# A buffer of its own for the second half of the first block's heads, and an early exponential

## The chip, the cores and the metric

The kernel runs on one core of one Trainium2 chip. The metric is the device time of one execution in microseconds (us). The engines are TensorE (PE in the rows, its weight loads PEld), VectorE (DVE), ScalarE (ACT), GpSimd (POOL) and SyncE (SP), whose queue issues all loads and stores here.

## The reference

Three layers follow each other on 8 batches of 576 tokens, all in float32:

```python
# 1: attention in chunks of 64 tokens, 8 heads of 64
scores = scale * q_c @ k_c^T
attn = exp(scores - max(scores)); attn /= sum(attn) + 1e-9
out = attn @ v_c                        # then heads side by side: x (B, S, 512)
# 2: feed-forward with a gate
h = relu(x @ w_in)                      # 1024 features
gate = sigmoid(conv over 3 tokens of h, with conv_w)
x = (h * gate) @ w_out
# 3: Fourier mixing
u = x + real(fft2(x));  un = (u - mean) / sqrt(var + 1e-6)
y = u + relu(un @ w_ch1) @ w_ch2
```

## The kernel before, in words

The 4608 tokens are cut into ten blocks, a first one of 256 tokens, eight of 512 and a last one of 256. For each block, `attention(i, q, ...)` (line 371) is called twice, for q = 0 and q = 1: each call covers half of the heads. It loads queries and keys, lets TensorE write the scores to PSUM (line 393), takes their maxima on VectorE (line 398) and turns them into a bias (line 399). ScalarE then runs one exponential for each of the n chunks and each of two groups, with the sum accumulated beside it (line 404; n is 4 in the first block and 8 in a wide one). VectorE adds the 1e-9, inverts the sums and scales the exponentials (lines 408 to 410), TensorE transposes them (line 419), ScalarE copies the result to `at` (line 422), and TensorE multiplies with the values (line 436). ScalarE copies that to `gl` in the first block (line 443).

The feed-forward layer goes feature group by feature group (`m_step`, eight groups f to a block): the linear step into PSUM (line 460 in the first block, in float32; line 469 later, with weights and data split in a high and a low part), ReLU to `h` (line 494), the convolution (lines 499 and 489) and the gate (line 506) in a tile `cv`, and the product `gh` (line 508). `x_step` multiplies with w_out (line 532 in the first block, line 538 later).

The weights are loaded as 64-bit words of 512 KB a tile and turned into float32 by one ScalarE instruction (line 293) and three of VectorE (lines 294 to 296). The wide tiles of the first loads lie in buffers that are used for other things later, so a row may call one `dd`, `fw` or `wide`, and the float32 result `t`, `u` or `f`. Splitting into high and low parts is lines 280 and 281.

Nothing in the program is issued in the order in which the Python code stands. Each step is an `op` with an engine, an estimated cost and a due time (`prio`). `Plan.emit` (line 156) runs a clock for each engine, and each time issues, of the steps that can start first, the one that is due first. Loads are given a time of arrival by bytes at 280 per ns, one behind the other (line 194), and TensorE costs are doubled in the first 30 us of that clock (line 190). The resulting order is fixed for each engine's queue; on the chip, engines work their queues in order and wait for each other.

A buffer (`buf(pool, tag, bufs, shape)`) is one use of a ring of `bufs` tiles with the same tag. A new use of a tile must wait for the readers of the use that lies `bufs` before it in that ring. Before the change, exponentials `es`, maxima `mx` and sums `sm` have rings of one tile each; `cv` has a ring of two tiles of 128 x 512.

Of the kernel before, what the change touches and what calls it, by code (L numbers as in the profile page):

```python
# [8 lines left out]
F32 = mybir.dt.float32  # L9
# [3 lines left out]
ACT = mybir.ActivationFunctionType  # L13
# [88 lines left out]
class Plan:  # L102
# [10 lines left out]
    def buf(self, pool, tag, bufs, shape, dtype=F32):  # L113
        return Buf(self, pool, tag, bufs, shape, dtype)

    def op(self, eng, cost, fn, prio, r=(), w=(), after=(), nbytes=0, spare=0):
        o = Op()
        o.spare = spare
        o.eng, o.cost, o.fn, o.prio, o.nbytes, o.seq = eng, cost, fn, prio, nbytes, len(self.ops)
        o.slots = [b for b in w if b.tag in self.ANY_ORDER and not b.writers]  # L120
        deps = {}
        for b in r:
            assert b.writers and not b.closed, b.tag
            for d in b.writers:
                deps[d] = True
        for b in w:
            assert not b.closed, b.tag
            if not b.writers:
                if b.pool in self.opened:
                    deps[self.opened[b.pool]] = True  # L130
                if b.before is not None:
                    for d in b.before.writers + b.before.readers:
                        deps[d] = True
                if b.previous is not None and b.previous not in w:
                    deps.setdefault(b.previous.writers[0], False)
            for d in b.writers + b.readers:
                deps[d] = True
        for d in after:
            deps[d] = True
        for b in r:  # L140
            for x in (b, b.base) if b.base else (b,):
                x.readers.append(o)
        for b in w:
            for x in (b, b.base) if b.base else (b,):
                x.writers.append(o)
        o.held = [b for b in {id(b): b for b in (*r, *w)}.values() if b.tag in self.ANY_ORDER]
        for b in o.held:
            b.left += 1
        o.deps, o.users = deps, []
        for d in deps:  # L150
            d.users.append(o)
        o.left, o.ready, o.end = len(deps), 0.0, None
        self.ops.append(o)
        return o
# [73 lines left out]
def kernel(  # L228
# [15 lines left out]
    pe, dve, act, pool, sp = nc.tensor, nc.vector, nc.scalar, nc.gpsimd, nc.sync  # L244
    plan = Plan()
    buf, op = plan.buf, plan.op
# [4 lines left out]
    const = ctx.enter_context(tc.tile_pool(name="const", bufs=1))  # L251
# [4 lines left out]
    pools["s"] = tc.alloc_tile_pool(name="seq", bufs=1, side="right")  # L256

    ident = const.tile([128, 128], F32, name="ident")

    def dram_buf(name, cols=512):  # L260
        b = buf("dram", name, 1, None)
        b.tile = dram.tile([128, cols], F32, name=name, tag=name)
        return b
# [6 lines left out]
    def load(dst, src, nbytes, prio, r=(), after=()):  # L270
        return op("SP", 450, lambda: sp.dma_start(out=dst(), in_=src()), prio, r=r, w=[dst], after=after, nbytes=nbytes)

    def vop(n, fn, prio, r, w, fast=False, scalars=0):
        return op("DVE", dve_cost(n, fast, scalars), fn, prio, r=r, w=w)

    def aop(n, fn, prio, r, w, psum=False, scalars=0, after=()):
        return op("ACT", act_cost(n, psum, scalars), fn, prio, r=r, w=w, after=after)
# [93 lines left out]
    def attention(i, q, prio, last):  # L371
        nw = SIZE[i] // 256
        n = 4 * nw
        blk = AT[i] // 256
        half = (slice(0, 64), slice(64, 128))
        qks, v = [], []
        for p in range(2):
            qks.append(buf(*(("s", "xlo", 2) if i + q == 1 and not i else ("a", "qk", 2)), [128, nw, 2, 256]))
            load(qks[p], lambda p=p: qk[blk:blk + nw, 2 * q + p].rearrange("w r a t -> r w a t"), 262144 * nw, prio - 12 + p)
        for p in range(2):  # L380
            v.append(buf("a", "v", 4, [128, nw, 256]))
            load(v[p], lambda p=p: v_in[blk:blk + nw, 2 * q + p].rearrange("w r t -> r w t"), 131072 * nw, prio - 10 + p)

        s = [buf("ps", "o" if i else "x", 4, [128, n, 64]) for _ in range(2)]

        def qk_unit():
            for w in range(nw):
                for j in range(2):
                    for p in range(2):
                        for u in range(2):  # L390
                            for h in range(2):
                                t, ks = qks[p](), slice(64 * (2 * j + u), 64 * (2 * j + u) + 64)
                                pe.matmul(s[h]()[half[u], 4 * w + 2 * p + j, :], t[half[h], w, 0, ks], t[half[h], w, 1, ks], start=True, stop=True)  # L393

        op("PE", 310 + 470 * nw, qk_unit, prio, r=qks, w=s)
        es, mx, sm = buf("a", "es", 1, [128, 2 * n, 64]), buf("a", "mx", 1, [128, 2, n]), buf("a", "sm", 1, [128, 2 * n, 1])
        for h in range(2):
            vop(64 * n, lambda h=h: dve.tensor_reduce(out=mx()[:, h, :], in_=s[h](), op=ALU.max, axis=AX.X), prio, [s[h]], [mx])
        vop(2 * n, lambda: dve.tensor_scalar(mx(), mx(), -0.125, None, op0=ALU.mult), prio, [mx], [mx])  # L399

        for h in range(2):
            def exp(ks, h=h):
                for k in ks:
                    act.activation(out=es()[:, n * h + k, :], in_=s[h]()[:, k, :], func=ACT.Exp, scale=0.125, bias=mx()[:, h, k:k + 1], accum_out=sm()[:, n * h + k, :])  # L404

            for ks in (range(k, k + 4) for k in range(0, n, 4)):
                op("ACT", 291 * 4, lambda exp=exp, ks=ks: exp(ks), prio, r=[s[h], mx], w=[es, sm])
        vop(2 * n, lambda: dve.tensor_scalar(sm(), sm(), 1e-9, None, op0=ALU.add), prio, [sm], [sm])
        vop(2 * n, lambda: dve.reciprocal(out=sm(), in_=sm()), prio, [sm], [sm])
        vop(128 * n, lambda: dve.tensor_tensor(es(), es(), sm().to_broadcast([128, 2 * n, 64]), op=ALU.mult), prio, [es, sm], [es])  # L410

        at = buf("a", "at", 2, [128, n, 128])
        for c in range(nw):
            tps = buf("ps", "o", 4, [128, 4, 128])

            def tr_unit(c=c, tps=tps):
                flat = es().rearrange("p a k -> p (a k)")
                for k in range(4):
                    pe.transpose(tps()[:, k, :], flat[:, 512 * c + 128 * k:512 * c + 128 * k + 128], ident)  # L419

            op("PE", 436, tr_unit, prio + 2, r=[es], w=[tps], spare=1)
            aop(512, lambda c=c, tps=tps: act.copy(out=at()[:, 4 * c:4 * c + 4, :], in_=tps()), prio + 2, [tps], [at], True)

        return lambda: values(i, q, nw, v, at, last)
# [616 lines left out]
    for q in range(2):  # L1041
        attention(0, q, -10 + q, -6 + q)()
# [8 lines left out]
    for i in range(NBLK):  # L1051
        t, u, step = place(i, 0), place(i + 1, 0) if i + 1 < NBLK else 0, SIZE[i] / 288
        if i + 1 < NBLK:
            rest = [attention(i + 1, q, *((t + (u - t) * (0.05 + 0.4 * q), u - 1.5 + 0.3 * q) if i else (t - 3.5 + 3 * q, t + 0.5 + 3 * q))) for q in range(2)]
            if not i:
                heads(1)
                for finish in rest:
                    finish()
# [54 lines left out]
    for c in range(NCH):  # L1113
        t = start + span * c
        begun = []
        for g in range(FG):
            begun.append(group(c, g, t + 7 * g))
            if (c, g) in LATE:
                n = LATE.index((c, g))
# [8 lines left out]
            second(c, j, t + 7 * (TILE0[c] // 2 + j), c + j == 0, c == NCH - 1 and j == HT[c] - 1)  # L1128

    with tc.manual_schedule():  # L1130
        make_identity(nc, ident)
        plan.emit()
        pools["e"].tile([128, 24], F32, tag="pad", name="pad", bufs=1)
        pools["e"].release()
        pools["b"].release()
# [109 lines left out]
```

## Time and profile before

| what | value |
|---|---|
| median of 3 runs | 1303.25 us (1302.99 to 1304.23) |
| the profiled execution | 1303.06 us |
| its span | 1301.3 us |
| TensorE busy | 1274.9 us, 98% |
| VectorE busy | 1036.1 us, 80% |
| ScalarE busy | 761.4 us, 59% |
| DMA | 206.16 MB, mean 158 GB/s |

The profiled execution's time is a little longer than its span, the time from the first to the last thing that the profiler saw. The busy time of an engine counts its instructions, not its waits. The chain that ended last is followed backwards from the last instruction, at each step to what released it or to the instruction before it on its engine. In a timeline, the bracket at a row's end gives the time that the engine sat idle before it, and what ended that.

### The profile page before, as it was taken

What the parts mean: (1) busy time and instruction counts of PE and PEld (TensorE: products, weight loads), DVE (VectorE), ACT (ScalarE), POOL (GpSimd) and SP (SyncE); (2) the same over time, 40 slices, a digit from 0 to 9 for tenths busy, and PEclk for the clock granted to TensorE, in tenths of its full rate; (3) what the DMA queues carried; (4) which work ended last, traced back from release to release, by engine and by line L of the source; (5) the groups of instructions that cost most, each with busy time, mean ns of one, the idle gap of its engine ahead of it and who ended that gap; (6) DMA issues with size and microseconds to landing.
All of it is one profiled execution on the core that took longest, in us unless ns stands there. A gap on an engine that the chain in (4) does not pass through costs nothing.

```text
span 1301.3 us, 24089 instructions
## 1 busy us (share of the span) xinstructions
PE 1274.9 (98%) x8880; PEld 1106.4 (85%) x8880; DVE 1036.1 (80%) x1909; ACT 761.4 (59%) x1902; POOL 112.3 (9%) x247
## 2 busy tenths in 40 slices
PE   5899999999999999999999999999999999999998
PEld 4788888888888888999999888888888888888887
DVE  5998878888786877887977757664599998998995
ACT  6887666768676665666756556566644334334331
POOL 0131212121030312210000000000000000000000
PEclk9999999999999999999999999999999999999999
DMA  9535242534413132258674866778655554554541
GB/s 339 178 108 175 78 129 90 187 100 158 135 57 103 34 98 62 63 172 267 203 238 144 255 182 204 214 238 273 200 159 165 176 168 146 173 171 141 174 140 41
DMA packets 155319, 206.16 MB, mean 158 GB/s; under 512 B 10304, under 2 KB 103104, under 8 KB 155200
## 3 DMA queue, kind: packets, MB, share of 16 engines
q1 hardware_dynamic: 155200, 204.61, 49.7%
q8 instruction: 70, 1.15, 0.4%
q14 instruction: 49, 0.40, 0.1%
HBM read 130.51 MB, written 74.06 MB: 157 GB/s over the span
## 4 chain that ended last, share of the span: by engine, by line
PE 93%; DVE 5%; ACT 1%; issue 1%; DMA 0%; SPq 0%; DVEq 0%; ACTq 0%
PE x L946 21%; PE x L1010 15%; PE x L538 15%; PE o L469 14%; PE o L1010 12%; PE o L946 4%; PE o L672 3%; PE o L705 2%; PE o L727 1%; PE o L436 1%; PE o L393 1%; PE o L844 1%; PE o L419 1%; ACT es L404 1%; DVE cv L489 0%
## 5 line engine op out<-in xcount | busy, mean ns | idle before, releaser
L946 PE MATMUL x<-sxh,t 128*128 128x512 f32 (+1 forms) x960 | 285.2, 369 | 1.1 <-ACT sum L929 0.6
L280 ACT CAST sxh<-raw 128x1024 fp32r<-128x1024 f32 (+1 forms) x143 | 144.9, 1029 | 201.7 <-DVE raw L856 84.3
L946 PEld LDWEIGHTS x<-sxh,t 128*128 128x128 f32 x960 | 177.9, 188 | 24.9 <-ACT sum L929 1.4
L946 PE MATMUL x<-sxl,t 128*128 128x512 f32 (+1 forms) x480 | 176.3, 367 | 0.0
L281 DVE TENSOR_TENSOR sxl<-raw,sxh 128x1024 fp32r<-128x1024 f32 (+1 forms) x143 | 168.7, 1192 | 9.5 <-ACT sxh L280 9.3
L469 PE MATMUL o<-x,wih 128*128 128x512 f32 (+1 forms) x576 | 172.2, 382 | 0.0
L489 DVE SCALAR_TENSOR_TENSOR cv<-h,cw,cv 128x512 f32<-128x512 f32 (+30 forms) x272 | 129.1, 495 | 31.9 <-ACT cv L499 31.6
L1010 PE MATMUL x<-t,sxh 128*128 128x512 f32 x576 | 144.4, 392 | 0.0
L469 PEld LDWEIGHTS o<-x,wih 128*128 128x128 f32 x576 | 104.6, 188 | 19.6
L1010 PEld LDWEIGHTS x<-t,sxh 128*128 128x128 f32 x576 | 103.7, 189 | 18.5
L538 PE MATMUL x<-gh,woh 128*128 128x512 f32 (+1 forms) x288 | 112.4, 390 | 0.0
L538 PE MATMUL x<-gh,wol 128*128 128x512 f32 (+1 forms) x288 | 109.3, 379 | 0.0
L538 PE MATMUL x<-gl,woh 128*128 128x512 f32 (+1 forms) x288 | 109.2, 379 | 0.0
L469 PE MATMUL o<-x,wil 128*128 128x512 f32 (+1 forms) x288 | 108.9, 378 | 0.0
L1010 PE MATMUL o<-t,sxh 128*128 128x512 f32 x432 | 108.3, 392 | 0.0
L946 PEld LDWEIGHTS x<-sxl,t 128*128 128x128 f32 x480 | 90.2, 188 | 11.2
L1010 PEld LDWEIGHTS o<-t,sxh 128*128 128x128 f32 x432 | 77.8, 189 | 13.9
L404 ACT ACTIVATE es<-o,mx 128x64 f32<-128x64 f32 x272 | 84.0, 358 | 8.9 <-DVE mx L399 8.9
L1030 DVE TENSOR_TENSOR u<-x,u 128x256 f32<-128x256 f32 x144 | 60.4, 422 | 29.9 <-PE x L1010 28.2
L856 DVE TENSOR_TENSOR raw<-raw 128x1024 f32<-128x1024 f32 (+1 forms) x70 | 84.0, 1202 | 0.1
L1010 PEld LDWEIGHTS x<-t,sxl 128*128 128x128 f32 x576 | 78.6, 190 | 5.6
L1010 PE MATMUL x<-t,sxl 128*128 128x256 f32 x576 | 80.5, 282 | 0.0
(263 smaller groups left out, 2394.1 us busy)
## 6 DMA issues: line engine op xcount, KB each, us to landing
raw<-h_scr SPq DMA_DIRECT2D x72, 512.0 KB, 4.6
h_scr<-sum SPq DMA_DIRECT2D x72, 256.0 KB, 3.3
u<-u_scr SPq DMA_DIRECT2D x66, 256.0 KB, 3.8
qk<-in_qk SPq DMA_DIRECT2D x32, 512.0 KB, 4.9
h_scr<-sum SPq DMA_DIRECT2D x48, 192.0 KB, 2.7
out_y<-u SPq DMA_DIRECT2D x35, 256.0 KB, 2.3
v<-in_v_in SPq DMA_DIRECT2D x32, 256.0 KB, 4.4
wide<-in_w_ch SPq DMA_DIRECT2D x16, 512.0 KB, 5.1
```

The costliest lines, as they stand in the source:

```text
L280: aop(n, lambda: act.copy(out=cut(h()), in_=cut(src())), prio, [src], [h], psum, after=after)
L281: vop(n, lambda: dve.tensor_tensor(cut(l()), cut(src()), cut(h()).bitcast(F32), op=ALU.subtract), prio, [src, h], [l])
L404: act.activation(out=es()[:, n * h + k, :], in_=s[h]()[:, k, :], func=ACT.Exp, scale=0.125, bias=mx()[:, h, k:k + 1], accum_out=sm()[:, n ...
L469: pe.matmul(acc(), w[:, ws], x, start=k == 0, stop=k == 11)
L489: vop(hi - lo, lambda: dve.scalar_tensor_tensor(cv()[:, lo:hi], in0=h()[:, off + k - 1 + lo:off + k - 1 + hi], scalar=tap(k), in1=cv()[:, ...
L538: pe.matmul(accs[d](), w[:, dsl], x, start=f == 0 and k == 0, stop=f == FT - 1 and k == 2)
L672: pe.matmul(acc()[:rows, :], x, w, start=k == 0 and n == 0, stop=k == 1 and n == 2)
L705: pe.matmul(accs[sine]()[:rows, :], w, x, start=n == 0, stop=n == len(todo) - 1)
L856: vop(n, lambda: dve.tensor_tensor(out(), x(), y(), op=alu), prio, r, w)
L946: pe.matmul(acc(), a, b, start=first and m == 0, stop=m == 5, skip_group_check=not first)
L1010: pe.matmul(acc()[:, :n], left[:, js], w()[:, cs], start=first and g == 0 and n == 512, stop=g == FG - 1 and n == 256, skip_group_check=True)
L1030: vop(256, lambda a=a, acc=accs[i], part=part, half=half: dve.tensor_tensor(part(us[a]()), acc()[:, half], part(us[a]()), op=ALU.add), t + ...
```

## The change

In the first block, the exponentials of the second call (q = 1) take their tile from the ring `cv` in place of the ring `es`; 128 x 8 x 64 elements are the size of a `cv` tile. The rings `mx` and `sm` have two tiles each, for all blocks. A one-column tile `unit` is added; it is zeroed by VectorE and put through an exponential on ScalarE, ahead of everything that the plan issues.

```diff
     ident = const.tile([128, 128], F32, name="ident")
+    unit = const.tile([128, 1], F32, name="unit")
...
-        es, mx, sm = buf("a", "es", 1, [128, 2 * n, 64]), buf("a", "mx", 1, [128, 2, n]), buf("a", "sm", 1, [128, 2 * n, 1])
+        es, mx, sm = buf("a", *(("cv", 2) if i == 0 and q else ("es", 1)), [128, 2 * n, 64]), buf("a", "mx", 2, [128, 2, n]), buf("a", "sm", 2, [128, 2 * n, 1])
...
     with tc.manual_schedule():
+        dve.memset(unit, 0.0)
+        act.activation(out=unit, in_=unit, func=ACT.Exp)
         make_identity(nc, ident)
         plan.emit()
```

## Rows read from the trace of the kernel before

**Rows 1.** The page: span, TensorE's busy time, the chain's shares by engine.
```profile
span 1301.3 us, 24089 instructions
...
PE 1274.9 (98%) x8880; PEld 1106.4 (85%) x8880; DVE 1036.1 (80%) x1909; ACT 761.4 (59%) x1902; POOL 112.3 (9%) x247
...
PE 93%; DVE 5%; ACT 1%; issue 1%; DMA 0%; SPq 0%; DVEq 0%; ACTq 0%
```

**Rows 2.** Busy time by stretch: PE, PEld, DVE, ACT, POOL (instructions), clock, DMA share, GB/s.
```profile
0.00:16.98 16.98, 5.04 (x100) 3.73 (x100) 5.36 (x18) 8.50 (x39) 0.70 (x6) 1.00 0.91 316
16.98:59.40 42.42, 35.62 (x477) 28.06 (x477) 39.98 (x85) 36.08 (x124) 5.10 (x7) 1.00 0.65 228
59.40:400.00 340.60, 340.43 (x2937) 286.18 (x2938) 283.41 (x583) 242.35 (x813) 70.56 (x141) 1.00 0.38 123
```

**Rows 3.** The chain that ended last, its beginning: start, us, engine and line.
```profile
5.11 0.75 DVE mx L398 x2
...
6.14 1.28 ACT L404
...
7.43 2.48 ACT es L404 x16
...
12.79 1.29 ACT es L404 x8
...
14.55 1.20 ACT es L404 x8
```

**Rows 4.** Timeline of ScalarE: start, us, line, operation, tiles, idle before.
```profile
12.79 0.31 ACT L404 ACTIVATE es<-x,mx 128x64 f32<-128x64 f32 x1 [2.33 <-PE o L419]
...
15.70 0.70 ACT L293 ACTIVATE wf<-dd 128x512 f32<-128x512 f32 x1
16.25 0.71 ACT L293 ACTIVATE wf<-fw 128x512 f32<-128x512 f32 x1
...
31.84 0.61 ACT L499 ACTIVATE cv<-h,cw 128x254 f32<-128x254 f32 x1
```

**Rows 5.** Timeline of VectorE.
```profile
10.02 0.42 DVE L398 TENSOR_REDUCE mx<-x 128x4 f32<-128x256 f32 x1
...
15.78 0.17 DVE L408 TENSOR_SCALAR sm<-sm 128x8 f32<-128x8 f32 x1 [2.60 <-ACT es L404]
...
16.99 0.42 DVE L294 TENSOR_SCALAR t<-wf 128x512 uint32<-128x512 uint32 x1
...
23.15 0.42 DVE L294 TENSOR_SCALAR f<-wf 128x512 uint32<-128x512 uint32 x1
```

**Rows 6.** Timeline of TensorE's matmuls (a float32 matmul leaves several records).
```profile
6.78 0.92 PE L393 MATMUL x<-xlo 64*64 64x64 f32 x24 [0.57 <-DMA xlo<-in_qk]
...
17.04 1.11 PE L419 MATMUL o<-ident,es 128*128 128x128 f32 x4 [1.30 <-DVE es L410]
18.12 1.22 PE L460 MATMUL o<-gl,t 128*128 128x256 f32 x2
...
21.48 1.22 PE L393 MATMUL o<-qk 64*64 64x64 f32 x64
...
23.60 1.89 PE L460 MATMUL o<-gl,u 128*128 128x256 f32 x8
...
59.39 1.97 PE L460 MATMUL o<-gl,dd 128*128 128x256 f32 x8 [0.76 <-DVE dd L296]
```

**Rows 7.** Issues of two w_out tiles (start, us), then their us to landing.
```profile
5.69 0.33 SPq L271 DMA_DIRECT2D dd<-in_w_out  x1
...
12.51 0.34 SPq L271 DMA_DIRECT2D dd<-in_w_out  x1
...
dd<-in_w_out SPq DMA_DIRECT2D x1, 512.0 KB, 6.9
...
dd<-in_w_out SPq DMA_DIRECT2D x1, 512.0 KB, 6.8
```

**Rows 8.** Busy time by stretch, columns as in rows 2.
```profile
564.00:572.00 8.00, 6.34 (x39) 5.91 (x38) 7.87 (x21) 3.46 (x10) 3.64 (x9) 0.79 0.18 66
```

## The prediction

> **What bounds the kernel now.** I read the page first: TensorE is busy 98% of the span, and 93% of the chain that ended last lies on it [rows 1]. The busy times by stretch then say where the missing 2% is: TensorE works 5.04 of the first 16.98 us and 35.62 of the next 42.42, but 340.43 of the 340.60 us after 59.40 [rows 2]. So 18.7 us of TensorE's idle time stands before 59.40. Behind that point the span is TensorE's own work, and a head that ends x us earlier ends the kernel x us earlier, unless a new wait takes it back.
>
> The chain of waits tells what holds the head. First come the scores of the first half of the heads, their maxima on VectorE, and then a table load of 1.28 us that stands alone on ScalarE, because it is queued in front of the first exponential and begins only with it; then eight pairs of exponential and accumulator read [rows 3]. The second half's exponentials start at 12.79 and not earlier, and ScalarE's timeline names the reason: 2.33 us of idle time, ended by TensorE's transposes of the first half, which had to read the one exponential tile before it could be overwritten [rows 4]. Its maxima stood at 10.02 behind the first half's last exponential, though its scores were done at 6.78 + 0.92 = 7.70 [rows 5, 6]. VectorE lost 2.60 us before the second half's sums at 15.78 and is full from there: 39.98 of 42.42 us [rows 2, 5]. TensorE's last early wait, at 59.39, is for VectorE's conversion of a weight [rows 6]. So the head is an in-order VectorE queue, and what counts is how much earlier it becomes full.
>
> **The change, part by part.**
> *The table load.* The memset and the exponential of a zero run before any query has landed; ScalarE's first 6.14 us are idle [rows 3]. They remove 1.28 us there. If that cover were gone, the load would cost what it costs now, so the bounds are 0 and a gain of 1.28; I take 1.28. The first half's exponentials then end at 7.43 + 2.48 - 1.28 = 8.63.
>
> *Own buffers for the second half.* Its maxima can follow its scores at 7.70. From scores to ScalarE's start the first half took 6.14 - 5.11 = 1.03 us [rows 3], so the second half is ready at about 8.78, 0.15 us behind the first half's end, where before it started at 12.79. Its eight exponentials take 1.29 + 1.20 us [rows 3], with a weight's conversion between them (0.55 us, the distance of two such starts, 15.70 and 16.25 [rows 4]). They end near 8.78 + 1.29 + 0.55 + 1.20 = 11.82, against 14.55 + 1.20 = 15.75 [rows 3]: 3.93 us earlier.
>
> *What is late next: landings.* After the copy of the first half's transposes (0.47 us, from 12.79 + 1.29 to 14.55 [rows 3]) ScalarE wants the first w_out tile at 12.3. That load is issued at 5.69 and lands 6.9 us later, at 12.59 [rows 7]; nothing in the change moves it. Its conversion starts near 12.64 where it started at 15.70 [rows 4]: 3.06 us earlier. A second check is the third w_out tile: issued at 12.51 when a buffer came free, landed at 19.3, used by VectorE at 23.15 [rows 5, 7]. Its issue can move by under 1 us, and the DMA engines are 91% busy in that stretch [rows 2], so I leave the landing; 0.7 us of conversion and 0.1 of hand-over later VectorE can take it at 20.1, again 3.05 us earlier. VectorE's own first conversion behind the heads, at 16.99, comes to 12.64 + 0.71 + 0.05 = 13.4, with about 0.4 us of small convolution-weight steps still owed (an estimate: a third of the 1.21 us between 15.78 and 16.99 [rows 5], where they stand now): 3.2 us. The smallest, 3.05, holds; I take 3.0.
>
> *Does it last to 59.4?* TensorE's pieces (transposes, values, the first linear steps) move with ScalarE's copies; in the old trace they wait for those. Order comes from the planner's own clock: by its line 194 block 1's queries arrive behind four query and four value tiles of 256 and 128 KB and five weight tiles; with their own two of 512 KB that is 5.3 MB, 18.8 us at 280 bytes per ns and near 21 us with the line's fixed terms, whatever the heads do. I expect the same order from there on. So the 3.0 us are carried to 59.39.
>
> *The new wait.* The second half's exponential tile comes from the convolution's ring of two, so the second feature's convolution writes the tile that the second half's transposes read. These end at 17.04 + 1.11 = 18.15 and would end near 14.6; that convolution writes at 31.84 [rows 4, 6]. 13 us hide it. Uncovered, it would stop ScalarE's queue, with the weight conversions behind it; cost 0.
>
> *Maxima and sums in two buffers, in every block, and the tiles' new addresses.* Behind 59.40 TensorE idles 0.17 us in 340 [rows 2], so there is nothing to win. The loss is bounded by reductions that VectorE now takes ahead of work for TensorE: two of 0.42 us in this block, some 0.7 for a wide one. No row shows such a case; between a gain of 0 and a loss of 1.4 I take 0, by the 0.17. No row shows what addresses do either; I put it at the same bounds and take 0.
>
> *TensorE's rate in the head.* The same linear step takes 1.22 us for two records at 18.12 and 1.89 for eight at 23.60 [rows 6]: 0.61 against 0.24 each, although the granted clock of both stretches is told as 1.00 [rows 2]. Between them TensorE worked without a gap from 17.04. With the change the same pieces come earlier but with gaps, so the slow rate may last longer. [...] The rows' own price is the second rival below.
>
> **Sum.** The profiled execution took 1303.06 us, 1.76 above its span, 0.19 below the median of the runs. 1303.06 - 3.0 = 1300.1 us.
>
> **The rivals.**
> 1. *The queue hides it* (the buffers don't do what they say). The planner could leave the second half's maxima behind the first half's sums, or put weight conversions before its exponentials; then only the table's 1.28 us remain: 1301.8. For it: the order is written by an estimate, not by the chip. Against it: the heads have the lowest due times of all.
> 2. *TensorE stays slow.* Of the first feature's eight records the last four ran fast; at 0.61 in place of 0.24 us they add 4 x 0.37 = 1.5 us before the first ReLU and, with block 1's scores (21.48 [rows 6]) next to them in the queue, before VectorE's next maxima. If none of it is hidden: 1303.06 - 3.0 + 1.5 = 1301.6.
> 3. *More comes.* If landings also move up, the 3.93 us are kept: 1299.1.
> 4. *Slower.* With a free buffer VectorE takes block 1's maxima before the weight steps that TensorE's linear steps wait for, as at 59.39, where one such wait costs 0.76 us [rows 6]. Block 1 has eight features: 8 x 0.76 = 6.1 us, 1303.06 - 3.0 + 6.1 = 1306.2. It decides from four of the eight on, which eat the 3.0. [...]
>
> **How the numbers follow.** Forecast 0.50 (own range 1299.4 to 1300.9), rival 1 0.12, rival 2 0.18, rival 3 0.11, rival 4 0.09. Some 0.2%, 2.6 us, is what a measurement of this kernel tells from no change; the border is at 1300.6. Faster: 0.45 of the forecast's 0.50, rival 3, and 0.01 of rival 2 make 0.57. Slower by 0.2% is most of rival 4, with an unnamed rest: 0.08. Same is what remains, 0.35. The range goes from below rival 3, 1298.6, to just above no change, 1303.4; that leaves out rival 4 and the rest beyond.
>
> **What would show it.** The table load before 3 us and exponentials from 6.15; the second half's from about 8.8 with no idle time ended by transposes; its sums near 11.9; the first w_out conversion at 12.6, waiting for its DMA; VectorE full from about 13.4; TensorE's last early wait at 56.4. If the second half starts at 8.8 and TensorE's last early wait still lies past 58, the gain was lost inside the head, and I am wrong in the step on order; if the head ends at 56.4 and the span doesn't shrink, wrong in the step that TensorE's work behind it is fixed.

## The result, and the profile after

The changed kernel takes 1315.21 us, the median of 5 runs (1314.4 to 1315.75), against 1303.25 before: a ratio of 1.009, 95% interval 1.0076 to 1.0105. It was forecast at 1300.1 and is 12.0 us slower than before. The profiled execution took 1315.75 us.

The page of the kernel after, in the lines of [rows 1]; its line numbers are one higher than before.

```profile
span 1314.0 us, 24076 instructions
...
PE 1288.4 (98%) x8880; PEld 1108.2 (84%) x8880; DVE 1038.4 (79%) x1910; ACT 763.6 (58%) x1903; POOL 113.0 (9%) x247
...
PE 93%; DVE 3%; ACT 2%; DMA 1%; issue 1%; SPq 0%; ACTq 0%; DVEq 0%
```

The span grew by 12.7 us, and TensorE's busy time by 13.5 with the same 8880 matmuls. So nearly all of the loss is TensorE's own work that takes longer, not time in which it waits. The stretches of [rows 2] (busy time of PE, PEld, DVE, ACT, POOL; clock; DMA share; GB/s), kernel after:

```profile
0.00:16.98 16.98, 7.64 (x122) 5.82 (x126) 8.23 (x24) 10.81 (x44) 0.70 (x6) 1.00 0.87 310
16.98:59.40 42.42, 35.19 (x475) 28.36 (x468) 38.93 (x83) 34.80 (x127) 6.63 (x9) 0.92 0.72 249
59.40:400.00 340.60, 339.95 (x2913) 283.06 (x2912) 281.41 (x574) 241.45 (x803) 69.58 (x139) 1.00 0.37 121
```

TensorE did gain 2.60 us of work before 16.98. Behind that the clock falls to a mean of 0.92, and after 59.40, at full clock and as good as always busy, TensorE shows 24 matmuls fewer in the same 340.60 us.

Where that comes from is read in the groups of matmuls by shape (line, engine, output and inputs, size of the weight tile and of the streamed tile, count | busy us, mean ns | idle before). Kernel before:

```profile
L946 PE MATMUL x<-sxh,t 128*128 128x512 f32 x576 | 182.3, 390 | 0.4 <-DVE u L921 0.4
L469 PE MATMUL o<-x,wih 128*128 128x512 f32 x512 | 160.5, 394 | 0.0
L1010 PE MATMUL x<-t,sxh 128*128 128x512 f32 x576 | 144.4, 392 | 0.0
L538 PE MATMUL x<-gh,wol 128*128 128x512 f32 x256 | 100.2, 391 | 0.0
L1010 PE MATMUL x<-t,sxl 128*128 128x256 f32 x576 | 80.5, 282 | 0.0
```

Kernel after:

```profile
L947 PE MATMUL x<-sxh,t 128*128 128x512 f32 x576 | 184.7, 394 | 0.4 <-DVE u L922 0.4
L470 PE MATMUL o<-x,wih 128*128 128x512 f32 x512 | 162.2, 398 | 0.6 <-DVE x L446 0.6
L1011 PE MATMUL x<-t,sxh 128*128 128x512 f32 x576 | 145.8, 395 | 0.0
L539 PE MATMUL x<-gh,wol 128*128 128x512 f32 x256 | 101.0, 395 | 0.0
L1011 PE MATMUL x<-t,sxl 128*128 128x256 f32 x576 | 79.9, 280 | 0.0
```

Every 512-column product became 3 to 4 ns longer, about 1%, in the feed-forward layer (lines 469 and 538) and in the Fourier layer (946 and 1010), parts of the program that the diff doesn't touch. The 256-column one became 2 ns shorter.

One point in each trace divides the loss: the last nine matmuls of line 672 with a 99-column tile and output `o`, shortly before the Fourier layer, against the end of the span. Their row before, after, and in the sixth experiment below (e6_moved; start, us, what), each from that kernel's TensorE timeline:

```profile
555.55 1.23 PE L672 MATMUL o<-dd,f 128*99 128x258 f32 x9
```
```profile
560.51 1.23 PE L673 MATMUL o<-dd,f 128*99 128x258 f32 x9
```
```profile
553.34 1.23 PE L675 MATMUL o<-dd,f 128*99 128x258 f32 x9
```

After is 4.96 us late there and 12.7 at the end. The sixth experiment is the whole change, in the same order, with those products' tiles at their old addresses: it is 2.21 early.

Now the head. ScalarE's timeline of the kernel after (start, us, line, operation, tiles, idle before):

```profile
0.73 1.28 ACT L1133 ACT_TABLE_LOAD   x1 [0.73 <-PEq L1235]
...
6.18 0.31 ACT L405 ACTIVATE es<-x,mx 128x64 f32<-128x64 f32 x1 [3.95 <-DVE mx L400]
...
9.65 0.31 ACT L405 ACTIVATE cv<-x,mx 128x64 f32<-128x64 f32 x1 [0.99 <-DVE sm L409]
...
13.02 0.72 ACT L294 ACTIVATE wf<-dd 128x512 f32<-128x512 f32 x1
...
20.47 0.68 ACT L294 ACTIVATE wf<-dd 128x512 f32<-128x512 f32 x1 [2.33 <-DMA dd<-in_w_out]
...
26.72 0.46 ACT L507 ACTIVATE cv<-cv 128x254 f32<-128x254 f32 x1
```

VectorE's:

```profile
8.60 0.76 DVE L399 TENSOR_REDUCE mx<-x 128x4 f32<-128x256 f32 x2 [2.52 <-PE x L394]
...
12.72 0.17 DVE L409 TENSOR_SCALAR sm<-sm 128x8 f32<-128x8 f32 x1
...
14.24 0.42 DVE L295 TENSOR_SCALAR t<-wf 128x512 uint32<-128x512 uint32 x1
...
21.18 0.43 DVE L295 TENSOR_SCALAR f<-wf 128x512 uint32<-128x512 uint32 x1 [0.26 <-ACT wf L294]
...
27.21 0.43 DVE L509 SCALAR_TENSOR_TENSOR gh<-cv,h 128x254 f32<-128x254 f32 x1 [1.62 <-ACT cv L507]
```

TensorE's, and behind it two of its stretches (columns as above):

```profile
7.63 0.92 PE L394 MATMUL x<-xlo 64*64 64x64 f32 x24 [0.51 <-DMA xlo<-in_qk]
...
18.20 1.10 PE L461 MATMUL o<-gl,u 128*128 128x256 f32 x4 [0.76 <-DVE u L297]
...
22.15 1.89 PE L461 MATMUL o<-gl,f 128*128 128x256 f32 x8
27.70 3.75 PE L533 MATMUL x<-gh,t 128*128 128x254 f32 x8 [3.66 <-DVE gh L509]
...
54.50 1.97 PE L461 MATMUL o<-gl,dd 128*128 128x256 f32 x8 [0.20 <-DVE dd L297]
```
```profile
24.00:28.00 4.00, 0.34 (x2) 0.31 (x2) 1.99 (x6) 3.88 (x25) 0.19 (x1) 0.82 1.06 382
28.00:30.00 2.00, 2.00 (x6) 1.57 (x6) 0.99 (x3) 2.00 (x13) 0.00 (x0) 0.50 1.00 379
```

Up to 21 us the head runs as forecast, only less far: VectorE's first weight step comes 2.75 us earlier, the one that waits for the third w_out tile 1.97 us earlier [rows 5]. About there the planner's order begins to differ from before. ScalarE's conversion of the fourth w_in tile moves back, from 27.26 us to 29.74, behind more of block 1's exponentials. So TensorE reaches the first `x_step` without the fourth linear step ahead of it, and stands still for 3.66 us until `gh` comes: VectorE waits for ScalarE's step on the gate in line 507, which stands in ScalarE's queue behind eight of those exponentials (as it does in before, where it starts at 28.96). In that pause the granted clock falls: it is 1.00 in 25 to 26 us, 0.77 in 26 to 27 and 0.50 from 27 to 32, and the eight products take 3.75 us, where eight of the same line at 46.07, with a clock of 1.00, take 1.98. Before had a pause at this place as well, a shorter one ahead of the fourth linear step, and its clock stayed at 1.00 from 24 to 40 us (TensorE's timeline before):

```profile
29.99 1.97 PE L460 MATMUL o<-gl,f 128*128 128x256 f32 x8 [2.77 <-DVE f L296]
```

The new order is not needed for that fall. In e5 and e7 below, whose order is before's, a pause of 2.1 us stands at the same place, the mean clock of 16.98 to 59.40 is 0.96, and the sixteen records of the linear step that read `f` take 508 ns in the mean; in e2, also in before's order, the pause is 2.2 us, the clock 1.00 and the mean 384 ns, as in before. So the length of the pause alone doesn't decide it.

### The profile page after: what moved, and what is told of

Same layout as the page of the kernel before. It is cut to its first block, busy times and chain, and to the rows that moved or that the text cites. A ratio compares the mean times of both kernels' runs of the same rounds, so it can differ in the third digit from the quotient of the medians.

```text
span 1314.0 us, 24076 instructions
## 1 busy us (share of the span) xinstructions
PE 1288.4 (98%) x8880; PEld 1108.2 (84%) x8880; DVE 1038.4 (79%) x1910; ACT 763.6 (58%) x1903; POOL 113.0 (9%) x247
## 4 chain that ended last, share of the span: by engine, by line
PE 93%; DVE 3%; ACT 2%; DMA 1%; issue 1%; SPq 0%; ACTq 0%; DVEq 0%
PE x L947 21%; PE x L1011 15%; PE x L539 15%; PE o L470 15%; PE o L1011 12%; PE o L947 4%; PE o L673 3%; PE o L706 2%; PE o L437 1%; PE o L728 1%; PE o L845 1%; PE o L394 1%; PE o L420 1%; ACT es L405 1%; DMA dd<-in_w_out 1%
## 5 line engine op out<-in xcount | busy, mean ns | idle before, releaser
L947 PE MATMUL x<-sxh,t 128*128 128x512 f32 (+1 forms) x960 | 288.1, 372 | 1.1 <-ACT sum L930 0.6
L282 DVE TENSOR_TENSOR sxl<-raw,sxh 128x1024 fp32r<-128x1024 f32 (+1 forms) x143 | 168.4, 1190 | 12.0 <-ACT sxh L281 11.9
L490 DVE SCALAR_TENSOR_TENSOR cv<-h,cw,cv 128x512 f32<-128x512 f32 (+31 forms) x272 | 128.6, 493 | 36.6 <-ACT cv L500 36.4
L1011 PEld LDWEIGHTS x<-t,sxh 128*128 128x128 f32 x576 | 103.2, 188 | 19.3
```

The lines of the kernel that those rows point to most:

```text
L282: vop(n, lambda: dve.tensor_tensor(cut(l()), cut(src()), cut(h()).bitcast(F32), op=ALU.subtract), prio, [src, h], [l])
L490: vop(hi - lo, lambda: dve.scalar_tensor_tensor(cv()[:, lo:hi], in0=h()[:, off + k - 1 + lo:off + k - 1 + hi], scalar=tap(k), in1=cv()[:, ...
L947: pe.matmul(acc(), a, b, start=first and m == 0, stop=m == 5, skip_group_check=not first)
L1011: pe.matmul(acc()[:, :n], left[:, js], w()[:, cs], start=first and g == 0 and n == 512, stop=g == FG - 1 and n == 256, skip_group_check=True)
```

## The experiments

The readings at the start: the bytes that the added tile takes shift the tiles that TensorE reads, and the shift makes the products longer; or the new order or the buffers' use makes them so, and addresses are innocent. A reserved tile moves everything that is allocated behind it on its side of the memory. In the built program `unit` takes 32 bytes; with it all tiles on the left side move by 32. (No trace shows an address; the distances are those of the built programs.) The second `mx` and `sm` move `x`, `gh` and, modulo 512, `gl` by 128 against the weights `wih`, `wil`, `woh`, `wol`. In the Fourier layer `t` lies on the right side of the memory, `sxh` and `sxl` on the left. All figures in one table; "moved" is the change against before, in bytes, in the distance of the two tiles that TensorE reads together (in the feed-forward layer `x`, `gh`, `gl` less the weights; in the Fourier layer `t` less `sxh`), then mean ns of the 512-column groups, median us, and the ratio to before with its interval (before was run again beside each round; its medians there are 1303.14 to 1303.32):

| kernel | moved | 469 wih | 538 wol | 946 sxh | 1010 sxh | us | ratio |
|---|---|---|---|---|---|---|---|
| before | 0; 0 | 394 | 391 | 390 | 392 | 1303.25 | |
| after | 128; -32 | 398 | 395 | 394 | 395 | 1315.21 | 1.009 [1.0076, 1.0105] |
| e1_unit64 | 128; -64 | 398 | 395 | 391 | 394 | 1309.12 | 1.0046 [1.0034, 1.0059] |
| e2_pad32 | 0; -32 | 394 | 392 | 394 | 395 | 1309.23 | 1.0045 [1.0032, 1.0057] |
| e3_table | 0; -64 | 394 | 391 | 391 | 394 | 1304.47 | 1.0007 [0.9998, 1.0016] |
| e4_buffers | 128; 0 | 398 | 395 | 390 | 392 | 1308.25 | 1.0038 [1.0026, 1.0051] |
| e5_gap128 | 128; 0 | 399 | 394 | 390 | 392 | 1308.71 | 1.004 [1.0027, 1.0052] |
| e6_moved | 0; 0 | 393 | 391 | 390 | 392 | 1301.94 | 0.999 [0.9981, 0.9999] |
| e7_both32 | 0; 0 | 394 | 392 | 390 | 392 | 1302.93 | 0.9998 [0.9989, 1.0007] |
| e8_table0 | 0; 0 | 394 | 391 | 390 | 392 | 1303.08 | 0.9998 [0.9989, 1.0007] |
| e9_x0only | x alone 128; +32 | 399 | 392 | 394 | 395 | 1312.11 | 1.007 [1.0055, 1.0085] |
| e10_gap1024 | 1024; +64 | 395 | 392 | 394 | 394 | 1309.27 | 1.0047 [1.003, 1.0064] |
| e11_gap512 | 512; +96 | 395 | 391 | 395 | 396 | 1311.68 | 1.0066 [1.0051, 1.0081] |
| e12_order | 0; 0 | 394 | 391 | 390 | 392 | 1300.61 | 0.998 [0.9971, 0.9989] |

**e1_unit64.** The change with a `unit` of 64 bytes, in the same order.

```diff
-    unit = const.tile([128, 1], F32, name="unit")
+    unit = const.tile([128, 16], F32, name="unit")
...
-        act.activation(out=unit, in_=unit, func=ACT.Exp)
+        act.activation(out=unit[:, 0:1], in_=unit[:, 0:1], func=ACT.Exp)
```

> The changed kernel with the one-column tile widened to 16 columns (64 bytes), of which one is used; the order of every engine's queue is the same. Theory A (place): the 4-byte tile takes 32 bytes and moves every tile of the left side from a multiple of 64 bytes to 32 behind one; 512-column matmuls are 1% slower for it. Then L947's sxh 128x512 group falls from 394 ns to 390, and the time by about 10 us to 1305; what is left against before is the head, +2 us. Theory B (the new order makes other engines disturb TensorE): nothing changes, 1315. Theory C (the early exponential does it): 1315.

None of the three came: half of the loss goes. Line 946 is down to 391 and the span to 1308.7, but the feed-forward products stay long. An address counts, and there is a second cause.

**e2_pad32.** Before, with a reserved tile that nothing uses.

```diff
+    unit = const.tile([128, 1], F32, name="unit")
```

> The kernel before with the one-column tile reserved and nothing done with it: all orders as before, the left side's tiles 32 bytes further on. Theory A: 512-column groups 1% slower (390 to 394 ns), 1313, about +10 us. Theories B and C: 1303, no change.

Four unused bytes a partition, 32 with what the allocation rounds to, cost 6.0 us: less than the 10 us expected of addresses alone. The groups of its trace, Fourier layer long, feed-forward as before:

```profile
L947 PE MATMUL x<-sxh,t 128*128 128x512 f32 x576 | 184.7, 394 | 0.4 <-DVE u L922 0.4
L470 PE MATMUL o<-x,wih 128*128 128x512 f32 x512 | 160.4, 394 | 0.0
L1011 PE MATMUL x<-t,sxh 128*128 128x512 f32 x576 | 145.8, 395 | 0.0
```

**e3_table.** Before, with the early exponential alone, on a 64-byte `unit`.

```diff
+    unit = const.tile([128, 16], F32, name="unit")
...
+        dve.memset(unit[:, 0:1], 0.0)
+        act.activation(out=unit[:, 0:1], in_=unit[:, 0:1], func=ACT.Exp)
```

> The kernel before with the early exponential alone, its tile 64 bytes wide, so that no tile leaves its multiple of 64; rings as before. Theory A: no 10 us; the table's 1.28 us come off the head, 1302.0. Theory C: 1313 or more. Theory B: 1302 to 1303.

No gain. The shift of 64 costs about 1 us in the Fourier layer (391 and 394), and ScalarE, done earlier with its exponentials, stops for a load (its timeline):

```profile
10.12 0.66 ACT L294 ACTIVATE wx<-dd 128x512 f32<-128x512 f32 x1 [1.35 <-DMA dd<-in_w_in]
```

**e4_buffers.** The change without `unit` and the exponential.

```diff
-        es, mx, sm = buf("a", "es", 1, [128, 2 * n, 64]), buf("a", "mx", 1, [128, 2, n]), buf("a", "sm", 1, [128, 2 * n, 1])
+        es, mx, sm = buf("a", *(("cv", 2) if i == 0 and q else ("es", 1)), [128, 2 * n, 64]), buf("a", "mx", 2, [128, 2, n]), buf("a", "sm", 2, [128, 2 * n, 1])
```

> The changed kernel without the one-column tile and its exponential: the new buffers and their order alone, tiles on multiples of 64. Theory A: no 10 us; the order's loss in the head stays, 1305 to 1306.5 (the table's 1.28 us back in the chain). Theory B: 1313 to 1315.

The Fourier layer is as before, and the feed-forward layer long: the second cause sits in the buffers. e5 asks if by their use or by their place.

**e5_gap128.** Before, with 128 unused bytes at the start of the pool that holds `x`, `gh` and `gl`.

```diff
+    pools["a"].tile([128, 32], F32, tag="gap", name="gap", bufs=1)
```

> The kernel before with 128 unused bytes at the start of the pool of the heads: weights (wih, wil, woh, wol) stay, and the tiles that stage 1 streams against them (x0, gh, gl) stand 128 bytes further on, as the two added tiles put them in the changed kernel. Order as before. Theory A2 (distance between the weight tile and the streamed tile): L469 wih 128x512 goes from 394 to 398 ns and L538 wol from 391 to 395; about +4.5 us, 1307.7. Theory B2 (stage 1 is slower by the new order of the other engines): 1303.2, groups as before.

By their place: nothing but the gap is added, and it costs 5.5 us.

```profile
L947 PE MATMUL x<-sxh,t 128*128 128x512 f32 x576 | 182.5, 390 | 0.4 <-DVE u L922 0.4
L470 PE MATMUL o<-x,wih 128*128 128x512 f32 x512 | 162.9, 399 | 0.0
...
L539 PE MATMUL x<-gh,wol 128*128 128x512 f32 x256 | 101.0, 394 | 0.0
```

**e6_moved.** The whole change, with `mx`, `sm` and `unit` in a pool above the others and a 128-byte gap in their old place, so that the tiles of the long products lie where they lay before.

```diff
+    pools["a"].tile([128, 32], F32, tag="gap", name="gap", bufs=1)
+    pools["m"] = tc.alloc_tile_pool(name="small", bufs=1)
...
-    unit = const.tile([128, 1], F32, name="unit")
+    unit = pools["m"].tile([128, 1], F32, tag="unit", name="unit", bufs=1)
...
-        es, mx, sm = buf("a", *(("cv", 2) if i == 0 and q else ("es", 1)), [128, 2 * n, 64]), buf("a", "mx", 2, [128, 2, n]), buf("a", "sm", 2, [128, 2 * n, 1])
+        es, mx, sm = buf("a", *(("cv", 2) if i == 0 and q else ("es", 1)), [128, 2 * n, 64]), buf("m", "mx", 2, [128, 2, n]), buf("m", "sm", 2, [128, 2 * n, 1])
...
-    turn("aw", "b", "left", end)
+    turn("maw", "b", "left", end)
```

> The whole change with its queue orders, but the maxima, sums and the one-column tile in a small pool above the heads, and 128 unused bytes in the heads' pool, so that wih, woh, x0, gh and all tiles of stage 3 stand where they stood before the change. Theory A2: both losses by place go; 394 and 391 ns in stage 1, 390 in stage 3; what is left is the head, 1303.2 to 1304.5. Theory B2: stage 1 stays slow, 1307.5 to 1309.

1301.94 us (11 runs, 1300.81 to 1303.84): 13 us faster than the change as it was, and ahead of before by 1.3, with an interval that just leaves out no change. All groups are at their old durations:

```profile
L949 PE MATMUL x<-sxh,t 128*128 128x512 f32 x576 | 182.3, 390 | 0.4 <-DVE u L924 0.4
L472 PE MATMUL o<-x,wih 128*128 128x512 f32 x512 | 159.6, 393 | 0.6 <-DVE x L448 0.6
L1013 PE MATMUL x<-t,sxh 128*128 128x512 f32 x576 | 144.4, 392 | 0.0
```

The head keeps its pause (TensorE's timeline):

```profile
26.89 3.34 PE L535 MATMUL x<-gh,t 128*128 128x254 f32 x8 [3.45 <-DVE gh L511]
```

**e7_both32.** e2's tile, and the tiles of the Fourier layer on the right side moved by 32 too: each tile elsewhere, their distance as before.

```diff
+    unit = const.tile([128, 1], F32, name="unit")
...
-        pools["e"].tile([128, 24], F32, tag="pad", name="pad", bufs=1)
+        pools["e"].tile([128, 16], F32, tag="pad", name="pad", bufs=1)
```

> The kernel before with all of its left side 32 bytes further on, as in the run with the reserved tile, and also the right side's tiles of stage 3 (t, u, raw) 32 bytes further on, by a smaller unused tile there. If it is the distance between two tiles that are read together, the 6 us go: 1303.2, L946 at 390 ns. If it is a tile's own place (off a multiple of 64 bytes), they stay or grow: 1309 or more.

The whole 6 us are gone again. What counts here is the distance, not where a tile lies: line 946 is at 390 ns again and line 1010 at 392. The feed-forward layer says the same in e2: there `x` and the weights moved by 32 together, and it kept its 394 and 392 ns.

```profile
L947 PE MATMUL x<-sxh,t 128*128 128x512 f32 x576 | 182.4, 390 | 0.4 <-DVE u L922 0.4
...
L1011 PE MATMUL x<-t,sxh 128*128 128x512 f32 x576 | 144.4, 392 | 0.0
```

**e8_table0.** e3, with `unit` above the other pools, so that no tile moves.

```diff
+    pools["m"] = tc.alloc_tile_pool(name="small", bufs=1)
+    unit = pools["m"].tile([128, 1], F32, tag="unit", name="unit", bufs=1)
...
-    turn("aw", "b", "left", end)
+    turn("maw", "b", "left", end)
...
+        dve.memset(unit, 0.0)
+        act.activation(out=unit, in_=unit, func=ACT.Exp)
```

> The kernel before with the early exponential alone, its one-column tile above the heads so that nothing else moves. All orders as before. Forecast of my prediction's first step: 1.28 us, 1301.9. Rival, from the run with the 64-byte tile: the first w_in tile's landing holds ScalarE's next instruction, so that at most a few tenths come through, 1302.9 to 1303.4; or TensorE's longer gap at 28 us costs its clock, 1303.5.

The table load by itself is worth nothing: 0.2 us, inside the interval. ScalarE's timeline shows where the gain goes in the head. The load leaves the path as forecast (it runs at 0.73), the exponentials start 1.27 us earlier, and then the queue stops for the w_in tile; the second half's exponentials still wait for the transposes and start at 13.03, not before the 12.79 of [rows 4]. The expectation's other rival is in this trace too: TensorE's pause ahead of the fourth linear step is 3.4 us, the mean clock of 16.98 to 59.40 is 0.96, and the sixteen records that read `f` take 476 ns in the mean, where before has 384.

```profile
6.16 0.31 ACT L406 ACTIVATE es<-x,mx 128x64 f32<-128x64 f32 x1 [3.93 <-DVE mx L401]
...
10.04 0.66 ACT L295 ACTIVATE wx<-dd 128x512 f32<-128x512 f32 x1 [1.40 <-DMA dd<-in_w_in]
13.03 0.31 ACT L406 ACTIVATE es<-x,mx 128x64 f32<-128x64 f32 x1 [2.33 <-PE o L421]
```

**e9_x0only.** Before, with the 128-byte gap directly ahead of `x`, so that `gh` and `gl` stay; the pad of the right side as in e7, which here moves the Fourier distance by +32.

```diff
+            if self.tag == "x000" and "gap" not in self.plan.opened:
+                self.plan.opened["gap"] = self.plan.pools["a"].tile([128, 32], F32, tag="gap", name="gap", bufs=1)
...
-        pools["e"].tile([128, 24], F32, tag="pad", name="pad", bufs=1)
+        pools["e"].tile([128, 16], F32, tag="pad", name="pad", bufs=1)
```

> The kernel before with 128 unused bytes ahead of x0 alone (weights, gh and gl stay), and the right side's tiles of stage 3 moved by 32 bytes while the left ones stay. Theory A2 (TensorE's two reads, weights and streamed tile): only the linear step with x0 slows, L469 from 394 to 398 ns, about 2.5 us, and L538 stays at 391; in stage 3 L946 goes to some 394, some 6 us; together 1311 to 1312. Rival D (any tile of the heads' pool against the rest, writes of other engines among them): both L469 and L538 slow or neither.

Only the product that reads `x` is long in the feed-forward layer (399 ns against 394); the one of `gl` and `gh` is not (392 against 391).

```profile
L471 PE MATMUL o<-x,wih 128*128 128x512 f32 x512 | 162.7, 399 | 0.0
...
L540 PE MATMUL x<-gh,wol 128*128 128x512 f32 x256 | 100.3, 392 | 0.0
```

**e10_gap1024 and e11_gap512.** e5 with a gap of 1024 and of 512 bytes. To make room, the right side's pad shrinks, which moves the Fourier distance by +64 and +96. The diff is e10's; e11 has 128 in place of 256, and no pad.

```diff
+    pools["a"].tile([128, 256], F32, tag="gap", name="gap", bufs=1)
...
-        pools["e"].tile([128, 24], F32, tag="pad", name="pad", bufs=1)
+        pools["e"].tile([128, 8], F32, tag="pad", name="pad", bufs=1)
```

> The kernel before with 1024 unused bytes at the start of the heads' pool, and stage 3's right side moved by 64 bytes. If the distance counts only within some power of two up to 1024 bytes, stage 1 is as before: 394 and 391 ns. If every other distance than the old one is slow, 398 and 395. Stage 3: a distance changed by -64 against +64 in the run with the 64-byte tile (391 and 394 ns for L946 and L1010); the same if only its size counts. Time 1303 to 1311.

> The kernel before with 512 unused bytes at the start of the heads' pool, and stage 3's right side moved by 96 bytes. If the distance counts only within 512 bytes (a slice of 128 weights), stage 1 is as before: 394 and 391 ns; if within 1024 or 2048 bytes, it may be slow or faster than before. Stage 3 by 96: no forecast from a theory, 390 to 396 ns. Time 1300 to 1311.

With 512 or 1024 bytes more, lines 469 and 538 are as in before (395 and 391 to 392), where 128 made them 399 and 394. So for these products a shift of 512 bytes is as good as none: the distance counts within 512 bytes. (256 was not tried, so it may repeat sooner.) Both kernels are slower for the Fourier layer alone: its products are long at +32, +64 and +96; at -64 line 946 pays only 1 ns (e1, e3), at -32 it pays 4 (e2). The pad that e7, e9 and e10 shrink and e11 drops is in the kernel before: a tile of 96 bytes on the right side that nothing reads. Its text thus held a sign that places may matter here.

**e12_order.** e6 with the exponentials of block 1's first half of heads due later.

```diff
-                op("ACT", 291 * 4, lambda exp=exp, ks=ks: exp(ks), prio, r=[s[h], mx], w=[es, sm])
+                op("ACT", 291 * 4, lambda exp=exp, ks=ks: exp(ks), prio + (4.5 if i == 1 and not q else 0), r=[s[h], mx], w=[es, sm])
```

> The kernel of e6_moved, with the exponentials of the first half of block 1's heads (block 0 is the first block) due 4.5 later in the planner than in e6_moved; nothing else is edited, and the tiles of the products of stages 1 and 3 stay at the old addresses. Theory (order in the head: in e6_moved TensorE waits 3.45 us for DVE's gh at 23.4 because ScalarE runs block 1's exponentials before the tanh, and the granted clock then falls to 0.50 in 28 to 30): the tanh comes earlier, the wait falls under 1.5 us, the clock stays at 1.00 in 28 to 32, the first matmul of stage 3 starts 1 to 2 us earlier than e6_moved's 574.90, and the time is 1300.0 to 1301.3. Rival (landings and DVE hold the head in any order): the wait goes elsewhere, 1301.5 to 1303.5.

1300.61 us, ratio to before 0.998 [0.9971, 0.9989], the fastest of all. Its time is the theory's, its trace the rival's: the pause is as long as in e6 (3.44 us against 3.45), only with another name, and the clock falls as it does there, to 0.50 in 28 to 30. TensorE's timeline and a stretch:

```profile
27.35 3.75 PE L463 MATMUL o<-gl,f 128*128 128x256 f32 x8 [3.44 <-DVE f L299]
```
```profile
28.00:30.00 2.00, 2.00 (x6) 1.59 (x5) 1.91 (x5) 1.97 (x11) 0.00 (x0) 0.50 1.03 420
```

The order is not shown to be the cause. The profiled execution was the slowest of eleven (1299.77 to 1303.88 us), with a mean clock of 0.996; the six at 0.998 or 0.999 took 1299.77 to 1301.34 us, five of 0.995 to 0.997 took 1300.34 to 1303.88. e6 spreads likewise: six runs at 0.996 or 0.997 took 1301.82 to 1303.84, five at 0.999 or 1.0 took 1300.81 to 1302.07. That e12 beats e6 by 1.3 us is no more than that spread. At like clock its medians are still 1.0 and 1.2 us lower, but the two were not run side by side: a small gain by the order is possible and not shown. What a head without the pause would bring stays open.

## Why the prediction was wrong

**The step that failed** is "Maxima and sums in two buffers, in every block, and the tiles' new addresses", of which it took the addresses at 0 with a bound of 1.4 us for the loss. They cost 11 to 13: the 32 bytes 1309.23 - 1303.25 = 6.0 (e2) and the 128 bytes 5.5 (e5), each alone; both together 1315.21 - 1301.94 = 13.3 (the change against e6). Without them the change is worth a gain of 1.3 (e6). The single prices less this gain make 10.2 of the 12.0. The counts agree: in the Fourier layer e2's 1008 products of 512 columns at line 947 with 4 ns each, 1008 at line 1011 with 3, 672 of 384 columns with 2, less 2 ns for 1008 of 256 columns, make 6.4 us, and from its first product on that layer took 724.2 us before and 730.5 in e2. The bound was drawn from reductions and idle time, that is from waits; it was not a bound on the duration of 8880 matmuls, of which 1 ns each is already 8.9 us. A price per instruction had to be bounded by the count of instructions. The prediction had named this case itself, as "wrong in the step that TensorE's work behind it is fixed": the wait that ended the head at 59.39 stands at 54.50 in the kernel after (a new one, of 0.57 us for `x`, comes at 63.67), and the span grew all the same.

The rest of the 12.0, 1.8 us, is not shown to be one thing or another. The trace after has one wait of 1.0 us at the start of the Fourier layer that before doesn't have (TensorE's waits in the kernel after: for what, us in total, times, longest):

```profile
PE o L728 <- ACT t L715: 1.0, 1, 1.0
```

and its first `x_step` starts at 27.70, where e6 has it at 26.89. But e1, in the same order, doesn't have that wait, so it may belong to this one execution, and that the two make 1.8 together may be chance.

**The table load: right in place, wrong in worth.** It ran at 0.73 and left the path. Its 1.28 us were taken as a gain (rival 1 prices them at 1301.8 for the whole kernel); alone it gives 0.2 (e8), not told from nothing, for ScalarE then waits for w_in, 1.40 us in that trace. The prediction looked for the next landing at w_out and passed over w_in.

**Own buffers: right, a little short.** The second half's exponentials start at 9.65, forecast 8.78 (its terms, 7.70 and 1.03, add up to 8.73), without the wait for the transposes: its scores ended at 8.55 instead of 7.70, since the load came 0.85 later in this execution. Sums at 12.72, forecast 11.9; first w_out conversion 13.02, forecast 12.6, and it waits for no load.

**Landings and "the same order from there on".** The third w_out tile's conversion waited 2.33 us for its load, as forecast, but till 20.47, where the landing was put at 19.3; VectorE took it at 21.18, forecast 20.1. So rival 3, that landings move up, did not come either. The order did not stay: TensorE runs four records of the second feature's step at 18.20, ahead of block 1's scores, and ScalarE's queue differs from 25 us on, with the pause at 24 to 27.7. Even so a gain arrives at the far end: in e6 TensorE is 2.21 us ahead at 553.34. With 2.2 in place of 3.0 the sum is 1300.9, and e6's profiled execution took 1300.81; but that was the fastest of its eleven, whose median is 1301.94, so the nearness is partly luck. The 3.0 was too high by 0.8 to 1.7.

**The new wait: right.** No wait of the convolution's steps on ScalarE for TensorE's transposes shows. Rival 1 (the queue hides it) did not come: the second half's maxima and exponentials moved up as above.

**Rival 2** (TensorE stays slow) came in another form: not as a slow start but as a clock of 0.50 after a pause, and not in every run (1.00 in before and e2). The start became fast sooner: four records of the linear step take 1.10 us at 18.20, where before took 1.22 for two at 18.12 and again at 20.33. That also answers why the clock in [rows 2] showed nothing of the slow records. The clock record of the trace begins only at 21.67 us in before and at 16.30 after, and a stretch without a record counts as 1.00; the matmuls are slow ahead of these points and fast behind them (in before two records of the linear step take 1.22 us at 20.33, four 1.13 at 22.63). The medians of the runs of lower and higher mean clock differ by 1.3 us in e6 and 1.6 in e12; what the fall costs as a whole is not measured, since e6's profiled execution, at 0.999, shows it too. In the trace after, TensorE worked 0.34 us of 24 to 28, and in 28 to 30 the clock is 0.50; in before it worked 0.01 us of 28 to 30, and the clock stayed at 1.00 up to 40. What makes the clock fall is not shown.

**Rival 4** named a slower end by VectorE's order. VectorE runs block 1's maxima between weight steps in both kernels, and TensorE idles 0.65 us in 340 after 59.40; it is not the cause. Nor does the lower clock of [rows 8], 0.79, show as a loss of time: in e8 the same stretch has a clock of 1.00, and the Fourier layer starts at 577.09 as it did before, at 577.08; VectorE, busy 7.87 us of 8 in both, holds it.

```profile
564.00:572.00 8.00, 5.91 (x42) 4.88 (x41) 7.87 (x21) 3.46 (x10) 3.62 (x9) 1.00 0.18 67
```

## What to carry to other kernels

A buffer that is added moves others. Where TensorE is the bound, list the tiles that it reads together in its largest groups, and after any change of allocation compare their mean durations by shape with the old trace: 1% there outweighs a whole head (here 13.3 us against a gain of 1.3). Put small new tiles where they move nothing (the end of a pool, or a pool of their own), or fill the gap to 512 bytes (which kept the feed-forward products at their old time here, 395 and 391 ns against 394 and 391, e11), and only then judge an edit.

## What the runs showed of the hardware

A 512-column float32 product takes 1 to 5 ns more or less with the distance between the two tiles that it reads (line 946: 390 ns in before, 391 in e1, 394 in e2, 395 in e11; in before and e2 with the same count and the same wait of 0.4 us); 32 bytes of it are worth 6.0 us of 1303 here (e2, undone by e7). In the feed-forward layer 128 bytes more make lines 469 and 538 399 and 394 ns (e5), while 512 or 1024 bytes more leave them at 395 and 391 to 392 (e11, e10), against 394 and 391 in before. It goes by the pair that is read together alone: with `x` moved and `gh` not, line 469 takes 399 ns and line 538 392 (e9). The Fourier layer's products of 256 columns stay or go 1 to 2 ns the other way (line 1010: 282 ns in before, 280 to 282 in the other runs). So the two tiles can't be placed without regard to each other. Why the distance matters was not tried, and which distance is best was not searched; before's may itself not be the best.
